# Weight-preparation jobs of the second layer in whole words, issued at the end of each tick

## The chip, the cores and the metric

The kernel runs on one core of one Trainium2 chip. The metric is the device time of one execution in microseconds (us). It uses TensorE (PE: matrix products; PEld: its weight loads), VectorE (DVE), ScalarE (ACT), GpSimd (POOL, almost unused) and SyncE (SP), whose queue issues every DMA.

## What is computed

Attention over short windows (chunks of 32 queries with 8 memory keys, 16 keys to the left, 8 to the right), then two feed-forward layers with all 3072 tokens:

```
x = attention(q, k, v, mem_k, mem_v)        # batch 4, 8 heads, 768 positions, head size 64
h = x @ w_in1;  x = softplus(h) @ w_out1    # 512 -> 2048 -> 512
h = x @ w_in2;  y = (h - tanh(h)) @ w_out2  # 512 -> 2048 -> 512
```

The weights come as 64-bit floats: in HBM each is two 32-bit words. The kernel makes a 32-bit float of the two words with integer and scaling steps, splits it in a high and a low part of a type that TensorE takes, and forms each product from three matmuls (high by high, high by low, low by high).

## The kernel before, in words

**Stages.** After an opening (the first four attention units, the first block of 512 tokens, the weights of layer 1), tokens 512 to 2047 pass layer 1 in three plain blocks: for each of 16 slices of the hidden size, `ff_h` (12 matmuls of 128x512), softplus and split (`chain1`), and, two slices later, `ff_y1` (12 matmuls). The remaining attention units run beside it. What is left (layer 1 for the last 1024 tokens, layer 2 for three groups of 1024) are four phases with a two-by-two scheme of seven products (Strassen's kind): `h_phase` is 56 groups of 6 matmuls, `y_phase` 56 groups of 6. In `y_phase` each group needs a fresh pair `gh`, `gl`: ACT casts a tile to `gh` (line 771), DVE subtracts to get `gl` (through `minus`, line 708); three such pairs can be in being at once. Here h0 and y0 are the two halves of the first phase, h1 and y1 of the second, and so on. The second phase is the first that uses the prepared weights of layer 2.

**Ticks.** `tick()` is called twice for each slice of the plain blocks and after every 12 matmuls in the phases, so a tick stands for 12 matmuls on PE, plus attention where there is any: an attention unit takes six ticks up to tick 60, then five up to tick 90. Plain blocks are ticks 0 to 97, h0 98 to 125, y0 126 to 153, h1 154 to 181, y1 182 to 209.

**Jobs.** Tables give the tick in which a job starts. A job is a generator: each tick takes it one step further. `JOBS_W1` (16 jobs) forms combinations of layer 1's weights. `JOBS_W2` (16 jobs, `job_w`) reads 1 MB of raw layer 2 weights, makes the floats, splits and stores seven combinations. `JOBS_X` (six jobs, `job_x`) reads layer 1's output, and stores seven split combinations; `JOBS_X1` is the like for layer 1. After its load, `job_w` waits `LEAD` ticks. Its steps then are: three ACT steps in one tick (lines 482, 485, 486: the low word to a 16-bit integer, the sign to a 16-bit float, the high word scaled), one DVE step that shifts and joins (488), an ACT cast of three of four parts (463), a DVE subtraction (467) and four sums (506 to 509), an ACT cast of four parts, and a DVE subtraction.

**Order.** Engines run their instructions in the order in which the program writes them. In `tick()` the jobs' steps (`active`) come before the attention's products, before softplus and cast of the current slice (`chain`), and before the copy `pT` of the transposed attention weights. Tiles named `o` rotate through four buffers: the jobs' split parts and the phases' results share them, and each is free again when its store has landed. Raw weights go to `w15`, `w6` or `w14`.

```
        active.extend(job() for job in plan.get(k, ()))
        for job in active[:]:
            if next(job, active) is active:
                active.remove(job)
        if r == 0 and before is not None:
            v_mm(before, ps_a)
```

Of the kernel before, what the change touches and what calls it, by code (L numbers as in the profile page):

```python
# [8 lines left out]
F32 = mybir.dt.float32  # L9
# [3 lines left out]
U16 = mybir.dt.uint16  # L13
F16 = mybir.dt.float16
AF = mybir.ActivationFunctionType
ALU = mybir.AluOpType
# [6 lines left out]
P = 128  # L23
# [11 lines left out]
N = 512  # L35
# [39 lines left out]
WPLACE = {q: i for i, q in enumerate((1, 2, 5, 6, 3, 7, 4))}  # L75
SHARED = {7: 7, 15: 7, 6: 14, 14: 14}
PLAIN = NB - 2
LEAD = 4
AHEAD = 3
GSLOT = (8, 9, 10, 11, 12, 13, 14, 7)  # L80
JOBS_W1 = (
    (0, "o", 7), (4, "i", 7), (8, "o", 6), (15, "i", 6), (19, "o", 0), (25, "i", 0), (30, "o", 1), (34, "i", 1),
    (40, "o", 2), (46, "i", 2), (50, "o", 3), (55, "i", 3), (60, "o", 4), (64, "i", 4), (68, "o", 5), (73, "i", 5),
)
JOBS_W2 = (
    (7, 15), (17, 15), (23, 6), (32, 15), (38, 6), (47, 15), (53, 6), (65, 15),
    (71, 6), (76, 15), (86, 15), (106, 14), (127, 15), (138, 15), (148, 15), (157, 14),
)
JOBS_X = (97, 114, 158, 168, 210, 220)
JOBS_X1 = (79, 91)  # L90
PHASES = ((1, NT - 1),) + tuple((2, b) for b in range(NT))
EXP_BIAS = 2.0 ** -112
SIGN_ONLY = 2.0 ** -100
LOW_EDGE = 2.0 ** -16
LOW_SCALE = 2.0 ** -29 * (1.0 - LOW_EDGE)
# [4 lines left out]
def attention_ffn_ffn(  # L100
# [10 lines left out]
    nc = tc.nc  # L111
    scale = 1.0 / float(D) ** 0.5

    const = ctx.enter_context(tc.tile_pool(name="const", bufs=1))
    wpool = ctx.enter_context(tc.tile_pool(name="w", bufs=1))
# [26 lines left out]
    low_bias = const.tile([P, 1], F32, name="low_bias")  # L142
# [74 lines left out]
    def run(steps):  # L217
        for _ in steps:
            pass
# [4 lines left out]
    def x_tile(j):  # L224
        if j not in xt:
            xt[j] = xpool.tile([P, KT, 2, N], F32R, name=f"x{j % 2}")
        return xt[j]
# [233 lines left out]
    def split_to(src, dst, shape):  # L461
        hi = opool.tile([P, *shape], F32R, name="o")
        nc.scalar.copy(out=hi, in_=src)  # L463
        yield
        put(hi, dst(0))
        lo = opool.tile([P, *shape], F32R, name="o")
        nc.vector.tensor_tensor(out=lo, in0=src, in1=hi.bitcast(F32), op=ALU.subtract)
        defer(put, lo, dst(1))
# [5 lines left out]
    def job_w(kind, p, slot):  # L474
        src = w2i if kind == "i" else w2o
        raw = wpool.tile([P, 4 * HALF, 2], U32, name=f"w{slot}")
        nc.sync.dma_start(out=raw.rearrange("p n two -> p (n two)"), in_=src[p].bitcast(U32))
        for _ in range(LEAD):
            yield
        lo, hi = raw[:, :, 0], raw[:, :, 1]  # L480
        x = raw.rearrange("p n two -> p (n two)").bitcast(U16).rearrange("p (n four) -> p n four", four=4)
        nc.scalar.activation(  # L482
            out=x[:, :, 0], in_=lo, func=AF.Identity, scale=LOW_SCALE, bias=low_bias
        )
        nc.scalar.mul(x[:, :, 1].bitcast(F16), hi.bitcast(F32), SIGN_ONLY)  # L485
        nc.scalar.mul(hi.bitcast(F32), hi.bitcast(F32), EXP_BIAS)
        yield
        nc.vector.scalar_tensor_tensor(
            out=hi, in0=hi, scalar=3, in1=lo, op0=ALU.logical_shift_left, op1=ALU.bitwise_or
        )  # L490
        yield
        w = raw.bitcast(F32)[:, :, 1].rearrange("p (i n) -> p i n", i=4)

        def place(s, a, n):
            return wid[p][:, a : a + n, s] if kind == "i" else wod[1][:, a : a + n, p, s]

        yield from split_to(
            w[:, 1:4], lambda s: ((0, 2, place(s, 0, 2)), (2, 1, place(s, 6, 1))), [3, HALF]
        )
        sums(w)  # L500
        yield
        yield from split_to(w, lambda s: ((0, 4, place(s, 2, 4)),), [4, HALF])

    def sums(w):
        add, sub = ALU.add, ALU.subtract
        nc.vector.tensor_tensor(out=w[:, 0], in0=w[:, 0], in1=w[:, 3], op=add)
        nc.vector.tensor_tensor(out=w[:, 1], in0=w[:, 0], in1=w[:, 1], op=sub)
        nc.vector.tensor_tensor(out=w[:, 2], in0=w[:, 2], in1=w[:, 1], op=sub)
        nc.vector.tensor_tensor(out=w[:, 3], in0=w[:, 3], in1=w[:, 1], op=sub)
# [68 lines left out]
        yield  # L578
        low(4, b21)

    def job_x(b, e):
        raw = wpool.tile([P, 2, 2, N], F32, name="w15")
        nc.sync.dma_start(out=raw, in_=y1d[b][e])
        for _ in range(LEAD):
            yield
        b11, b21, b12, b22 = raw[:, 0, 0], raw[:, 0, 1], raw[:, 1, 0], raw[:, 1, 1]
        o = {}

        def high(q, src):
            if b and q in (2, 5, 7):  # L590
                h, l = (gpool.tile([P, N], F32R, name=n) for n in ("gh", "gl"))
                stores = [(x2d[b][q - 1][:, e, s], t) for s, t in enumerate((h, l))]
            else:
                t = opool.tile([P, 2, N], F32R, name="o")
                h, l = t[:, 0], t[:, 1]
                stores = [(x2d[b][q - 1][:, e], t)]
            o[q] = h, l, src, stores
            nc.scalar.copy(out=h, in_=src)

        def low(q):  # L600
            h, l, src, stores = o.pop(q)
            minus(l, src, h.bitcast(F32))
            for place, t in stores:
                defer(nc.sync.dma_start, place, t.bitcast(F32))

        high(1, b11)
        high(2, b21)
        yield
        low(1)
        low(2)  # L610
        minus(b12, b12, b11)
        high(3, b22)
        yield
        low(3)
        minus(b22, b22, b12)
        high(5, b12)
        yield
        low(5)
        minus(b11, b22, b11)
        high(6, b22)  # L620
        yield
        low(6)
        minus(b21, b21, b22)
        high(7, b11)
        yield
        low(7)
        high(4, b21)
        yield
        low(4)
# [77 lines left out]
    def minus(out, x, y):  # L707
        nc.vector.tensor_tensor(out=out, in0=x, in1=y, op=ALU.subtract)  # L708
# [118 lines left out]
    slot = 0  # L827
# [7 lines left out]
    plan, now, active, late = {}, [0], [], []  # L835
# [2 lines left out]
        plan.setdefault(t, []).append(lambda x=(kind, p): job_w1(*x))  # L838
    for (t, slot), w in zip(JOBS_W2, W2):
        plan.setdefault(t, []).append(lambda x=(*w, slot): job_w(*x))  # L840
    for n, t in enumerate(JOBS_X):
        plan.setdefault(t, []).append(lambda x=(n // 2, n % 2): job_x(*x))
    for n, t in enumerate(JOBS_X1):
        plan.setdefault(t, []).append(lambda n=n: job_x1(n))
    starts = {t: i for i, t in enumerate((*ATT_TICKS, AT_END))}
# [3 lines left out]
    def defer(f, *args, more=0):  # L849
        late.append((now[0] + more, f, args))  # L850

    def tick(chain=iter(())):
        k = now[0]
        now[0] += 1
        calls, late[:] = [x for x in late if x[0] <= k], [x for x in late if x[0] > k]
        for _, f, args in calls:
            f(*args)
        if k in starts:
            place[:] = starts[k], k
        i, r = place[0], k - place[1]  # L860
        u = ATT_ORDER[i] if i < len(ATT_ORDER) else None
        before = ATT_ORDER[i - 1] if 0 < i <= len(ATT_ORDER) else None
        if u is not None:
            if r == 1:
                if i + 2 < len(ATT_ORDER):
                    qk_load(ATT_ORDER[i + 2])
                if 0 < i < len(ATT_ORDER) - 1:
                    v_load(ATT_ORDER[i + 1])
                next(soft[u])
            elif r == 2:  # L870
                run(soft.pop(u))
        if r == 1 and before in VIA_DRAM:
            run(soft.pop(("x", before)))
        active.extend(job() for job in plan.get(k, ()))
        for job in active[:]:
            if next(job, active) is active:
                active.remove(job)
        if r == 0 and before is not None:
            v_mm(before, ps_a)
        if r == 0 and u is not None:  # L880
            s_mm(u, ps_a)
        if r == 4 and u is not None:
            t_mm(u, ps_a[:, 0, :])
        next(chain, None)
        if r == 4 and u is not None:
            t_out(u)
        next(chain, None)
        if r == 0 and before is not None:
            soft["x", before] = (x_out if before // UB < PLAIN else x_out_whole)(before)
            next(soft["x", before])  # L890
        if r == 0 and u is not None:
            soft[u] = softmax(u)
            next(soft[u])
        if r == 0 and before is not None:
            next(soft["x", before], None)
        run(chain)

    with tc.manual_schedule(engines={mybir.EngineType.PE}):

# [9 lines left out]
        if True:  # L909
# [6 lines left out]
            for name in ORDER.split():  # L916
                kind, i = name.rstrip("0123456789"), int(name.lstrip("qkviow"))
# [23 lines left out]
            for token in OPENING.split():  # L941
                op = token[:2] if token[0] == "c" else token.rstrip("0123456789")
                i = int(token[len(op) :])
# [5 lines left out]
                elif op == "Z":  # L949
                    for _ in range(i):  # L950
                        nc.tensor.matmul(
                            out=ps_h[1], lhsT=zeros[:, :P], rhs=zeros, start=True, stop=True
# [23 lines left out]
                else:  # L976
                    if op == "y":
                        going["w", i] = split_w(raws[str(i)], i)
                    elif op[0] == "y":
                        k = "io".index(op[1])  # L980
# [8 lines left out]
        for j in range(1, PLAIN):  # L989
            x = x_tile(j)  # L990
# [108 lines left out]
```

## Time and profile before

| | |
|---|---|
| median of three runs | 1093.36 us (1091.57 to 1097.41) |
| profiled execution: its own time | 1098.39 us |
| profiled execution: span, first to last instruction | 1096.5 us |
| PE / DVE / ACT busy | 1054.6 / 751.5 / 677.2 us |
| mean granted TensorE clock | 0.978 of full speed |
| DMA | 319.99 MB, mean 292 GB/s |

The page is of one execution. Its own time is 1.9 us more than its span, and 5.0 us more than the median of the three runs. Busy time of PE counts a product from its start to its modelled end, so it overlaps its neighbours; what PE loses is better read from the distance between rows of the same work.

### The profile page before, as it was taken

To read this page: it belongs to the slowest core of one execution; us is meant where nothing else is said; L and a number is where in the kernel's file an instruction comes from. 1 tells how busy PE (TensorE), PEld (TensorE's weight loads), DVE (VectorE), ACT (ScalarE), POOL (GpSimd) and SP (SyncE) were. 2 spreads that over 40 slices of the span, in tenths; PEclk is the share of its full clock that TensorE was granted. 3 is DMA by queue.
4 is the path that set the end of the run, shared out by engine and by line. 5 is a ranking of instruction groups with operands and counts; after the bars stand their busy time and mean duration, and the time that the engine had idled before them with its cause. 6 is when DMAs were issued, how large, how long until landed. Compare 5 with 4: busy or idle time off the path is not lost.

```text
span 1096.5 us, 18583 instructions
## 1 busy us (share of the span) xinstructions
PE 1054.6 (96%) x7322; PEld 858.3 (78%) x7322; DVE 751.5 (69%) x1199; ACT 677.2 (62%) x982; POOL 7.5 (1%) x14
## 2 busy tenths in 40 slices
PE   7999999998999988999988998999999999999998
PEld 5787888887787866878866776878888888888887
DVE  7997557667686564555675667887678677455876
ACT  6996566977787785557566574555455554344553
POOL 1000000000000000000000000000000000000000
PEclk8999999999899898999998998999999999999999
DMA  9999877797799873699987999988889878655661
GB/s 378 408 323 328 287 255 243 245 342 257 269 312 320 296 241 130 240 392 341 371 321 298 362 350 356 332 320 306 314 290 375 313 289 327 233 199 211 217 215 68
DMA packets 112231, 319.99 MB, mean 292 GB/s; under 512 B 8464, under 2 KB 67344, under 8 KB 93712
## 3 DMA queue, kind: packets, MB, share of 16 engines
q1 hardware_dynamic: 112144, 318.80, 81.1%
q8 instruction: 58, 0.95, 0.3%
q14 instruction: 29, 0.24, 0.1%
HBM read 220.73 MB, written 98.04 MB: 291 GB/s over the span
## 4 chain that ended last, share of the span: by engine, by line
PE 80%; ACT 10%; DVE 5%; DMA 3%; issue 2%; SPq 0%; ACTq 0%; DVEq 0%
PE ps_y L404 40%; PE ps_h L404 24%; PE ps_b L404 12%; ACT w L482 2%; ACT w L485 2%; PE ps_a L367 2%; PE ps_a L286 1%; DMA wod<-o 1%; DMA x<-wid 1%; PE ps_a L338 1%; ACT o L463 1%; DVE w L708 1%; ACT t L427 1%; ACT gh L771 1%; ACT gh L439 1%
## 5 line engine op out<-in xcount | busy, mean ns | idle before, releaser
L771 ACT CAST gh<-w 128x512 fp32r<-128x512 f32 x224 | 138.9, 624 | 137.7 <-DVE gl L708 99.9
L708 DVE TENSOR_TENSOR gl<-w,gh 128x512 fp32r<-128x512 f32 x236 | 162.7, 691 | 77.1 <-ACT gh L771 71.7
L404 PE MATMUL ps_h<-x,w 128*128 128x512 f32 x756 | 183.3, 393 | 0.1
L404 PE MATMUL ps_y<-gh,w 128*128 128x512 f32 x512 | 174.9, 404 | 0.0
L404 PEld LDWEIGHTS ps_h<-x,w 128*128 128x128 f32 x756 | 142.1, 189 | 30.2 <-ACT t L427 0.2
L404 PE MATMUL ps_y<-w,x 128*128 128x512 f32 x504 | 122.7, 396 | 3.7 <-ACT kept L699 3.7
L404 PE MATMUL ps_y<-gh,x 128*128 128x512 f32 x384 | 119.5, 389 | 0.4 <-ACT gh L771 0.4
L404 PEld LDWEIGHTS ps_y<-w,x 128*128 128x128 f32 x504 | 96.5, 192 | 24.8 <-ACT kept L699 4.5
L404 PEld LDWEIGHTS ps_y<-gh,w 128*128 128x128 f32 x512 | 98.1, 192 | 21.9 <-issue 0.2
L404 PE MATMUL ps_y<-gl,w 128*128 128x512 f32 x256 | 101.4, 396 | 0.0
L404 PEld LDWEIGHTS ps_y<-gh,x 128*128 128x128 f32 x384 | 72.1, 188 | 15.7 <-ACT gh L771 0.8
L735 ACT ACTIVATE tanh<-sum 128x512 f32<-128x512 f32 x72 | 45.3, 633 | 57.5 <-DVE sum L704 57.4
L404 PE MATMUL ps_b<-gh,x 128*128 128x512 f32 x192 | 75.0, 390 | 4.0 <-ACT gh L771 4.0
L404 PE MATMUL ps_y<-gl,x 128*128 128x512 f32 x192 | 74.9, 390 | 0.2 <-DVE gl L708 0.2
L444 DVE TENSOR_TENSOR gl<-t,gh 128x512 fp32r<-128x512 f32 x64 | 45.5, 714 | 43.1 <-ACT gh L439 42.9
L404 PE MATMUL ps_h<-gh,x 128*128 128x512 f32 x192 | 74.9, 390 | 0.0
L404 PE MATMUL ps_b<-w,x 128*128 128x512 f32 x252 | 64.3, 391 | 2.1 <-ACT kept L699 1.3
L708 DVE TENSOR_TENSOR w<-w 128x512 f32<-128x512 f32 x88 | 60.4, 688 | 6.6 <-ACT w L427 5.4
L404 PE MATMUL ps_h<-w,x 128*128 128x512 f32 x252 | 64.1, 390 | 0.3 <-DMA x<-wid 0.3
L427 ACT ACTIVATE t<-ps_h 128x512 f32<-128x512 f32 x64 | 38.1, 596 | 39.6 <-PE ps_h L404 36.2
L704 DVE TENSOR_TENSOR sum<-ps_y,kept 128x512 f32<-128x512 f32 x48 | 32.9, 690 | 41.7 <-PE ps_y L404 32.1
L404 PEld LDWEIGHTS ps_b<-w,x 128*128 128x128 f32 x252 | 47.1, 188 | 13.0 <-ACT kept L699 2.2
(161 smaller groups left out, 1720.5 us busy)
## 6 DMA issues: line engine op xcount, KB each, us to landing
x<-wod SPq DMA_DIRECT2D x48, 1024.0 KB, 5.0
x<-wid SPq DMA_DIRECT2D x24, 1024.0 KB, 7.2
w<-x2d SPq DMA_DIRECT2D x21, 1024.0 KB, 7.3
x<-wid SPq DMA_DIRECT2D x24, 768.0 KB, 6.8
wod<-o SPq DMA_DIRECT2D x32, 512.0 KB, 5.8
wid<-o SPq DMA_DIRECT2D x32, 512.0 KB, 5.5
qk<-in_qk SPq DMA_DIRECT2D x21, 768.0 KB, 6.4
x2d<-o SPq DMA_DIRECT2D x30, 512.0 KB, 8.8
```

Of the source, the lines that this page charges most:

```text
L286: nc.tensor.matmul(out=ps[cc, j, KEYS * p : KEYS * (p + 1)], lhsT=a["q"][r, p, cc], rhs=a["k"][r, c, p, :], start=True, stop=True,)
L338: nc.tensor.transpose(ps[:, p * P : (p + 1) * P], a["sm"][:, p * P : (p + 1) * P], ident)
L367: nc.tensor.matmul(out=ps[h : h + 64, p % 2, 2 * P + t0 : 2 * P + t0 + CHUNK], lhsT=v, rhs=pT, start=True, stop=True,)
L404: nc.tensor.matmul(out=ps, lhsT=a, rhs=b, start=first and i == 0, stop=last and i == 2, skip_group_check=on,)
L427: nc.scalar.activation(out=out, in_=x, func=AF.Softplus)
L444: eng.tensor_tensor(out=gl, in0=t, in1=gh.bitcast(F32), op=ALU.subtract)
L482: nc.scalar.activation(out=x[:, :, 0], in_=lo, func=AF.Identity, scale=LOW_SCALE, bias=low_bias)
L485: nc.scalar.mul(x[:, :, 1].bitcast(F16), hi.bitcast(F32), SIGN_ONLY)
L704: nc.vector.tensor_tensor(out=h, in0=ps, in1=t, op=ALU.add)
L708: nc.vector.tensor_tensor(out=out, in0=x, in1=y, op=ALU.subtract)
L735: nc.scalar.activation(out=t, in_=h, func=AF.Tanh)
L771: nc.scalar.copy(out=gh, in_=src)
```

## The change

Each raw pair of words is now made to a float by two ACT steps and two DVE steps, one in each of four ticks, all on whole 32-bit words: ACT turns the low word to its three bits in place; DVE joins the sign bit from the high word to it; ACT scales the high word; DVE shifts it and joins the two. The wait after a load is three ticks and not four, for `job_x` too. A further tick without a step stands between the first split and the second. The jobs' block moves to the end of `tick()`. The tables get new ticks, and `job_x` and one `job_w` other raw buffers (`w7`, `w10`).

```
-LEAD = 4
+LEAD = 3
...
 JOBS_W2 = (
...
-    (71, 6), (76, 15), (86, 15), (106, 14), (127, 15), (138, 15), (148, 15), (157, 14),
+    (67, 6), (73, 15), (90, 10), (96, 15), (107, 14), (111, 15), (127, 15), (149, 15),
 )
-JOBS_X = (97, 114, 158, 168, 210, 220)
+JOBS_X = ((85, 15), (105, 7), (157, 7), (163, 15), (210, 15), (220, 15))
...
         lo, hi = raw[:, :, 0], raw[:, :, 1]
-        x = raw.rearrange("p n two -> p (n two)").bitcast(U16).rearrange("p (n four) -> p n four", four=4)
-        nc.scalar.activation(
-            out=x[:, :, 0], in_=lo, func=AF.Identity, scale=LOW_SCALE, bias=low_bias
+        nc.scalar.activation(out=lo, in_=lo, func=AF.Identity, scale=LOW_SCALE, bias=low_bias)
+        yield
+        nc.vector.scalar_tensor_tensor(
+            out=lo, in0=hi, scalar=0x80000000, in1=lo, op0=ALU.bitwise_and, op1=ALU.bitwise_or
         )
-        nc.scalar.mul(x[:, :, 1].bitcast(F16), hi.bitcast(F32), SIGN_ONLY)
+        yield
         nc.scalar.mul(hi.bitcast(F32), hi.bitcast(F32), EXP_BIAS)
         yield
         nc.vector.scalar_tensor_tensor(
...
         sums(w)
+        yield
         yield
...
-    def job_x(b, e):
-        raw = wpool.tile([P, 2, 2, N], F32, name="w15")
+    def job_x(b, e, slot):
+        raw = wpool.tile([P, 2, 2, N], F32, name=f"w{slot}")
...
-        active.extend(job() for job in plan.get(k, ()))
-        for job in active[:]:
-            if next(job, active) is active:
-                active.remove(job)
         if r == 0 and before is not None:
             v_mm(before, ps_a)
...
         run(chain)
+        active.extend(job() for job in plan.get(k, ()))
+        for job in active[:]:
+            if next(job, active) is active:
+                active.remove(job)
```

One thing more follows from the code. The loops that fill the plan use the name `slot`, which also numbers the plain blocks' two PSUM banks; it leaves them at 14 before and at 15 now, so the first plain slice takes bank `ps_h[1]` and not `ps_h[0]`, and all later slices swap too.

**ACT in y0.** The order of ACT's instructions around the job that starts in tick 127, before (its raw tile is `w_5621`; `gh` are the casts that PE waits for, `kept` copies of finished products):

```order
L699 COPY kept<-ps_h_81 128x512
L771 CAST gh<-w_5271 128x512
L771 CAST gh<-w_5280 128x512
L771 CAST gh<-w_5419 128x512
L482 ACTIVATE w_5621<-w_5621,low_bias 128x1024
L485 ACTIVATE w_5621<-w_5621 128x1024
L486 ACTIVATE w_5621<-w_5621 128x1024
L771 CAST gh<-w_5428 128x512
```

and now (raw tile `w_5669`; line 773 is the line 771 of before, 487 is 486):

```order
L773 CAST gh<-w_5317 128x512
L481 ACTIVATE w_5669<-w_5669,low_bias 128x1024
L773 CAST gh<-w_5326 128x512
L773 CAST gh<-w_5478 128x512
L773 CAST gh<-w_5487 128x512
L773 CAST gh<-w_5572 128x512
L487 ACTIVATE w_5669<-w_5669 128x1024
L773 CAST gh<-w_5572 128x512 x3
```

Three job steps stood between two casts; now one does, twice, with four casts between them.

**ACT in the plain blocks.** The same around the ninth of these jobs (started in tick 71 before, 67 now), which falls beside attention (`t` is softplus, `pT` the copy that the attention's last products wait for, `o<-c` a step of a `JOBS_W1` job). Before:

```order
L427 ACTIVATE t<-ps_h_82 128x512
L350 COPY pT<-ps_a 128x512
L439 CAST gh<-t 128x512
L482 ACTIVATE w_4128<-w_4128,low_bias 128x1024
L485 ACTIVATE w_4128<-w_4128 128x1024
L486 ACTIVATE w_4128<-w_4128 128x1024
L463 CAST o<-c_4177 128x1024
L387 COPY x_3903<-ps_a 128x2x2x128
```

Now:

```order
L387 COPY x_3911<-ps_a 128x2x2x128
L463 CAST o<-w_3735 128x1024
L481 ACTIVATE w_3972<-w_3972,low_bias 128x1024
L327 ACT_TABLE_LOAD
L327 ACTIVATE sm<-sm 128x512
L427 ACT_TABLE_LOAD
L427 ACTIVATE t<-ps_h_82 128x512
L439 CAST gh<-t 128x512
L487 ACTIVATE w_3972<-w_3972 128x1024
L463 CAST o<-c_4113 128x1024
```

The attention's copy to `x` now stands ahead of the jobs' steps of its tick, and the two conversion steps are a tick's work apart.

**DVE in y0.** What DVE gets for it around the same job of y0 (`gl` is the subtraction that PE waits for). Before:

```order
L708 TENSOR_TENSOR gl<-w_5419,gh 128x512
L708 TENSOR_TENSOR gl<-w_5428,gh 128x512
L708 TENSOR_TENSOR w_5519<-w_5280 128x512
L708 TENSOR_TENSOR gl<-w_5518,gh 128x512
L488 SCALAR_TENSOR_TENSOR w_5621<-w_5621 128x1024
```

Now:

```order
L710 TENSOR_TENSOR gl<-w_5478,gh 128x512
L483 SCALAR_TENSOR_TENSOR w_5669<-w_5669 128x1024
L710 TENSOR_TENSOR gl<-w_5487,gh 128x512
L710 TENSOR_TENSOR w_5573<-w_5326 128x512
L710 TENSOR_TENSOR gl<-w_5572,gh 128x512 x2
L710 TENSOR_TENSOR w_5573<-w_5478 128x512
L710 TENSOR_TENSOR gl<-w_5572,gh 128x512
L798 TENSOR_TENSOR o<-ps_b_4861,kept 128x512
L489 SCALAR_TENSOR_TENSOR w_5669<-w_5669 128x1024
```

One step of 1024 elements has become two, with seven instructions of the phase between them.

## Rows read from the trace of the kernel before

**Rows 1.** The page: span, and busy time of each engine.

```profile
span 1096.5 us, 18583 instructions
...
PE 1054.6 (96%) x7322; PEld 858.3 (78%) x7322; DVE 751.5 (69%) x1199; ACT 677.2 (62%) x982; POOL 7.5 (1%) x14
```

**Rows 2.** Busy by stage: window, length, PE, PEld, DVE, ACT, POOL; granted clock, DMA share, GB/s.

```profile
127.00:324.00 197.00, 192.38 (x2060) 157.53 (x2042) 135.37 (x245) 146.47 (x161) 0.00 (x0) 0.98 0.81 276
324.00:455.00 131.00, 121.10 (x1183) 98.97 (x1174) 81.37 (x143) 92.34 (x108) 0.00 (x0) 0.95 0.70 237
455.00:532.00 77.00, 76.60 (x336) 62.47 (x335) 41.74 (x65) 48.37 (x78) 0.00 (x0) 1.00 0.98 363
532.00:625.00 93.00, 83.86 (x340) 65.97 (x339) 63.92 (x100) 54.36 (x72) 0.00 (x0) 0.94 0.90 333
625.00:711.00 86.00, 80.36 (x340) 65.29 (x339) 62.52 (x99) 54.88 (x83) 0.00 (x0) 0.96 0.95 349
```

**Rows 3.** The chain of waits in order of time: start us, length us, what.

```profile
127.19 2.99 PE ps_y L404 x12
...
146.13 2.96 PE ps_y L404 x12
...
324.10 2.97 PE ps_y L404 x12
...
513.48 19.04 PE ps_y L404 x84
...
625.14 19.04 PE ps_y L404 x84
...
710.65 1.38 PE ps_y L404 x6
...
1016.65 76.17 PE ps_y L404 x336
```

**Rows 4.** Timeline of PE: the first group of h0.

```profile
454.92 1.53 PE L404 MATMUL ps_b<-w,ring 128*128 128x512 f32 x6
```

**Rows 5.** Timeline of ACT in y0: start, length; in brackets idle before, releaser.

```profile
549.40 2.60 ACT L482 ACTIVATE w<-w,low_bias 128x1024 uint16<-128x1024 uint32 x1
552.03 2.48 ACT L485 ACTIVATE w<-w 128x1024 f16<-128x1024 f32 x1
...
555.55 1.65 ACT L771 CAST gh<-w 128x512 fp32r<-128x512 f32 x3
```

**Rows 6.** Timeline of PE at the same place.

```profile
556.21 0.50 PE L404 MATMUL ps_b<-gh,x 128*128 128x512 f32 x1 [3.29 <-ACT gh L771]
```

**Rows 7.** Groups by line and shape: count, busy us, mean ns, idle before.

```profile
L482 ACT ACTIVATE w<-w,low_bias 128x1024 uint16<-128x1024 uint32 x16 | 41.9, 2621 | 1.0 <-DMA w<-in_w2o 1.0
L485 ACT ACTIVATE w<-w 128x1024 f16<-128x1024 f32 x16 | 40.3, 2516 | 0.5
...
L488 DVE SCALAR_TENSOR_TENSOR w<-w 128x1024 uint32<-128x1024 uint32 x16 | 19.6, 1223 | 26.8 <-ACT w L486 26.8
...
L486 ACT ACTIVATE w<-w 128x1024 f32<-128x1024 f32 x16 | 18.1, 1129 | 0.5
...
L467 DVE TENSOR_TENSOR o<-w,o 128x768 fp32r<-128x768 f32 x16 | 15.2, 952 | 0.3
...
L506 DVE TENSOR_TENSOR w<-w 128x256 f32<-128x256 f32 x16 | 6.7, 420 | 0.0
...
L177 ACT ACTIVATE c<-w,low_bias 128x1024 uint16<-128x1024 uint32 x4 | 5.8, 1453 | 0.0
```

**Rows 8.** The loads of raw weights (line 477): time from issue to landing.

```profile
DMA to landing us min/median/max: 6.6/8.6/11.4
```

**Rows 9.** Timeline of ACT late in y0: a job's cast that waits for a store.

```profile
607.47 1.12 ACT L463 CAST o<-w 128x1024 fp32r<-128x1024 f32 x1 [3.98 <-DMA wod<-o]
```

**Rows 10.** Waits of PE: total us, times, longest us.

```profile
PE ps_a L338 <- DVE sm L333: 8.0, 5, 2.9
```

**Rows 11.** Five microseconds of y0 (columns as in rows 2).

```profile
580.00:585.00 5.00, 5.00 (x23) 4.13 (x22) 3.54 (x6) 3.25 (x6) 0.00 (x0) 1.00 1.01 428
```

More of the change, by code (lines that the diff above doesn't have):

```diff
@@ L81 @@
 JOBS_W1 = (
-    (0, "o", 7), (4, "i", 7), (8, "o", 6), (15, "i", 6), (19, "o", 0), (25, "i", 0), (30, "o", 1), (34, "i", 1),
-    (40, "o", 2), (46, "i", 2), (50, "o", 3), (55, "i", 3), (60, "o", 4), (64, "i", 4), (68, "o", 5), (73, "i", 5),
+    (0, "o", 7), (4, "i", 7), (8, "o", 6), (12, "i", 6), (16, "o", 0), (20, "i", 0), (24, "o", 1), (29, "i", 1),
+    (35, "o", 2), (40, "i", 2), (44, "o", 3), (48, "i", 3), (52, "o", 4), (61, "i", 4), (70, "o", 5), (75, "i", 5),
 )
 JOBS_W2 = (
-    (7, 15), (17, 15), (23, 6), (32, 15), (38, 6), (47, 15), (53, 6), (65, 15),
-    (71, 6), (76, 15), (86, 15), (106, 14), (127, 15), (138, 15), (148, 15), (157, 14),
+    (5, 15), (17, 15), (23, 6), (31, 15), (38, 6), (46, 15), (51, 6), (60, 15),
+    (67, 6), (73, 15), (90, 10), (96, 15), (107, 14), (111, 15), (127, 15), (149, 15),
 )
-JOBS_X = (97, 114, 158, 168, 210, 220)
+JOBS_X = ((85, 15), (105, 7), (157, 7), (163, 15), (210, 15), (220, 15))
 JOBS_X1 = (79, 91)
@@ L840, in attention_ffn_ffn @@
         plan.setdefault(t, []).append(lambda x=(*w, slot): job_w(*x))
-    for n, t in enumerate(JOBS_X):
-        plan.setdefault(t, []).append(lambda x=(n // 2, n % 2): job_x(*x))
+    for n, (t, slot) in enumerate(JOBS_X):
+        plan.setdefault(t, []).append(lambda x=(n // 2, n % 2, slot): job_x(*x))
     for n, t in enumerate(JOBS_X1):
```

## The prediction

> **What bounds the kernel now.** The page comes first: PE is busy for 1054.6 of 1096.5 us, ACT for 677.2 and DVE for 751.5 [rows 1]. So only PE can be the bound as a whole, and 1096.5 - 1054.6 = 41.9 us of idle is what one sees at once. It isn't all that PE loses. The table by stage shows where: in the plain blocks, in y0 and in h1 PE has 4.6, 9.9, 9.1 and 5.6 us idle, and in the same four stages the granted clock is 0.94 to 0.98, while h0 stands at 1.00 with 0.4 us idle [rows 2]. A clock below 1.00 as a mean of a stage is time at the lower of its two levels (1.2 GHz in place of 2.4): products run, but slower.
>
> To have both losses in one number I use the pace of undisturbed work. The last half phase is 336 matmuls in 76.17 us [rows 3], so 0.227 us each, 2.72 us for a tick's 12, 76.17 us for each half phase. Against that:
> - Plain blocks: from 127.19 to the start of h0 at 454.92 [rows 3, 4] are 327.7 us. Without loss they are ten attention units of six ticks, 146.13 - 127.19 = 18.94 each; six of five ticks, one tick less, 16.22 each; and at the end seven groups of 12 matmuls, 19.0. That makes 305.7. Lost: 22.0. By tick 60 (324.10 in place of 127.19 + 189.4 = 316.6) 7.5 of it have gone, the rest after.
> - h0: 454.92 to 532.52 (513.48 + 19.04): 77.6, lost 1.4. y0: to 625.14, 92.6, lost 16.4. h1: to 710.65, 85.5, lost 9.3 [rows 3, 4].
> - The next four halves: 710.65 to 1016.65 are 306.0, against 304.7: lost 1.3. The last half loses nothing.
>
> In all 22.0 + 1.4 + 16.4 + 9.3 + 1.3 = 50.4 us: idle, and the slow clock behind it.
>
> **What causes it.** One place in y0 shows the pattern: ACT runs lines 482 and 485 from 549.40, then 486, and casts the next `gh` only at 555.55: a hold of 6.15 us [rows 5]. PE starts again at 556.21, after 3.29 us of idle whose releaser is that `gh` [rows 6]. So in y0 a hold of about 6.15 - 3.29 = 2.9 us is covered by the pairs that are ready, and what is over it, PE pays. The three steps cost 2621 + 2516 + 1129 = 6266 ns by their means, in 16 jobs [rows 7]. The two that write 16-bit halves of words take more than twice the one that writes whole words, for 1024 elements each.
>
> **The change part by part.** *Removed:* lines 482 and 485, 5.14 us of ACT per job. *Added:* one ACT step from integer words to integer words, in place, and one DVE step. The trace has no ACT step of this form. From below, the nearest is line 486, also whole words in place: 1.13 us; a step of less is excluded since it handles as many elements. From above it is line 482 itself, same function and input: 2.62 us; in between stands line 177, which writes the same integers to another tile: 1.45 us [rows 7]. I take 1.2, near 486, because the two rows at 2.5 share only the half-word writing in place. By the Trainium skill (ScalarE: Activation LUTs, "What ACT_TABLE_LOAD costs") an activation with a bias tile takes some 280 + 0.833 x 1024 = 1133 ns, whatever the type: an estimate that leaves my sum as it is. For the half-word steps the trace contradicts it, 2621 measured; were it right there too, the old burst would be some 3.4 us and hardly worth breaking up.
>
> So a job's conversion takes 1.2 + 1.13 = 2.3 us of ACT in place of 6.3, in two ticks. The longest hold by one conversion step falls from 6.3 to 1.2 us, well under the 2.9 of cover. DVE gains 1.22 us per job (as line 488 [rows 7]), 16 x 1.22 = 19.6 us over the kernel, beside 345 us in which it is idle.
>
> *Moved to the end of the tick:* softplus, casts, `pT` and the attention's copies no longer stand behind the jobs' steps of the same tick. In the plain blocks this takes from attention the waits that came through ACT. The price is that jobs run a little later; all that they make is stored ticks before it is read (the last `JOBS_W2` job ends in tick 161, and y1, its reader, starts in tick 182), so I cost this at nothing. The same holds for the additional empty tick.
>
> *Three ticks after a load instead of four:* three ticks are 8.2 us, loads land after 6.6, 8.6 and 11.4 us (least, median, most) [rows 8]. ACT may so be held between 0 and 3.2 us per job, 0.4 at the median. That is at the 2.9 us of y0 in the worst case and nearly always under it: between 0 and 16 x 0.3 = 5 us; I take 1.
>
> *New ticks and buffers.* Jobs leave y0: three started there, now two, one of them with all but two steps in h1. h0 gets more: `JOBS_W2` jobs from 96, 107 and 111 and one `job_x`, where one and two were. In h0 ACT is idle for 28.6 and DVE for 35.3 of 77 us [rows 2], so it has room. The other PSUM bank for the first plain slice costs nothing: between the last use of that bank and the first slice PE has the groups Y12 and Y13 of the opening, 5.4 us, to hide one softplus; without them it would be less than a microsecond, once.
>
> *What is late next.* Three kinds of wait remain. A job's second cast waits for an `o` whose store hasn't landed: 3.98 us at 607.47 [rows 9], over the cover; the empty tick (2.7 us) takes most of it, but h1 holds a `JOBS_W2` job and two `job_x` end to end. DVE's longest step is still a subtraction and four sums in one tick, 0.95 + 4 x 0.42 = 2.6 us [rows 7]. And attention waits for DVE's `sm`, 8.0 us in five places [rows 10]. I leave 1.5 us in the plain blocks, 2 in y0 (the load's 1 in it) and 2 in h1; 1.4 of h0 and 1.3 behind y1's start stay, since nothing there is taken away.
>
> **Sum.** Recovered: 22.0 - 1.5 = 20.5; 16.4 - 2 = 14.4; 9.3 - 2 = 7.3; together 42.2. The profiled execution took 1098.4, which gives **1056.2**. Its time was 5.0 above the median of 1093.4; the work without loss, 1098.4 - 50.4 = 1048.0, is the same in each run, so I take the runs' spread for spread of the stalls that go, and forecast **1056 us** for the median.
>
> **Rivals.**
> 1. *The integer step costs 2.6 us after all* (what is slow is the integer input or being in place). For it: line 482 has both. Against: line 485 has no integer and is as slow. Then one hold of 2.6 us per job, just under the cover; with a cast or a store behind it some spill, up to 1 us for half of the 16 jobs: 1058 to 1064. Chance 0.12.
> 2. *DMA bounds h0.* It moved 363 GB/s x 77 us = 28.0 MB [rows 2]. By the tile shapes a `JOBS_W2` job is 2.9 MB and a `job_x` 4.7, so two jobs and a half more and one `job_x` less add about 2.9: 30.9 MB in 76.2 us, 405 GB/s. Five microseconds of y0 reached 428 [rows 11], so it can fit, but stores will land later, and `o` waits with them. If it holds only 363, h0 takes 30.9 / 0.363 = 85 us, 9 more than its products: 1060 to 1068. Chance 0.17. By the Trainium skill (DMA: Bandwidth & Descriptors, "Where 436 GB/s comes from") HBM gives a core some 358 GB/s: h0 would then take 86 us, 10 more than its products. The 428 of rows 11 speak against that as a ceiling here.
> 3. *DVE becomes the wait.* Jobs now overlap in the plain blocks, and a tick can hold a first split (2.6 us) beside the four sums of a `JOBS_W1` job (1.7): 4.3 us in ticks 13 and 25, with little less in 71, 75 and 81. `sm` comes late, at up to 2.9 us [rows 10] in each of five places: 14.5, less the 1.5 already left in, 1069. For it: DVE is the busiest engine after PE. Against: two ticks lie between attention's DVE steps and PE's use. Chance 0.10.
> 4. *Slower: each load holds ACT.* With three ticks' lead, the first conversion step waits at the head of ACT's queue, now without other work between. Once loads take over 8.2 + 6.3 - 1.2 = 13.3 us, the hold is longer than today's burst and every stall is back, larger. At 17 us the hold is 10 us, 3.7 more than now, in 16 jobs 59 us more: about 1150. It decides from 13.3 us; the longest landing now is 11.4 [rows 8]. Chance 0.03.
> 5. *The stalls hardly move,* because each only passes to the next engine in its chain: 1090 to 1096. Against: rows 5 and 6 name one cause. Chance 0.02.
>
> **How the numbers follow.** The forecast has 0.56, with a range of its own of 1049 to 1062 (nothing left of the losses in y0, h1 and the plain blocks gives 1050.7, the runs' spread a little less). About 0.5% (5.5 us) is what a measurement of this kernel can tell from no change. Faster by that: forecast and rivals 1 to 3, 0.95; same 0.02; slower 0.03. For eight in ten the range starts at 1047 and takes in rivals 1 and 2 and rival 3: to 1073.
>
> **What would show it.** Right: the new ACT step at 1.1 to 1.5 us; no wait of PE on `gh`, `pT` or `kept` over 1 us in y0, h1 or the plain blocks; the granted clock at 1.00 in the plain blocks from the second on and in y0 and h1; y0 and h1 at 76 to 79 us; the plain blocks, tick 0 to h0, at about 307. Wrong: h0 over 80 us with casts that wait for stores (rival 2); PE waiting for `sm` over 10 us in all (rival 3); ACT waiting for raw loads at the step (rival 4).

## The result, and the profile after

The changed kernel takes 1057.18 us (median of four runs, 1054.88 to 1057.76) against 1093.41 before (median of four runs too): a ratio of 0.966, 95% interval 0.963 to 0.969. The forecast was 1056, with a range of 1047 to 1073. The profiled execution took 1054.88 us with a span of 1053.1, against 1098.39 and 1096.5. The two profiled executions lie 43.5 us apart and the medians 36.2: the one before was 5.0 above its median, this one is 2.3 below. Stage by stage the text reads the profiles.

The page after, in the lines that answer to [rows 1], and the granted clock in 40 slices:

```profile
span 1053.1 us, 18599 instructions
...
PE 1034.4 (98%) x7320; PEld 846.0 (80%) x7322; DVE 768.8 (73%) x1215; ACT 615.8 (58%) x966; POOL 7.9 (1%) x14
...
PEclk9999999999999999999999999999999999999999
```

ACT lost 61.4 us of work, DVE gained 17.3. PE's idle time fell from 41.9 to 18.7 us, and the granted clock is 0.9 or more in each of the 40 slices.

The chain of waits in order of time, at the places of [rows 3] (start, length, what):

```profile
125.21 2.99 PE ps_y L404 x12
...
494.17 19.04 PE ps_y L404 x84
...
590.41 19.04 PE ps_y L404 x84
...
668.43 76.16 PE ps_y L404 x336
...
973.24 76.17 PE ps_y L404 x336
```

The timeline of PE has h0's first group, as [rows 4] before:

```profile
430.57 1.52 PE L404 MATMUL ps_b<-w,ring 128*128 128x512 f32 x6
```

By the pace used in the prediction (305.7 us from tick 0 to h0, 76.2 for each half phase) the plain blocks now take 305.4 and lose nothing; h0, to 494.17 + 19.04 = 513.21, takes 82.6 and loses 6.4; y0 takes 77.2 and loses 1.0; h1 78.0, 1.8; the four halves after it 304.8, 0.1. Losses before were 22.0, 1.4, 16.4, 9.3 and 1.3. So 50.4 us of loss have become 9. Another 2 us lie ahead of tick 0, which starts at 125.21 and not at 127.19; in the kernels below it starts at 125.0 to 127.5, with the change or parts of it, so these 2 us are chance. Four of the five stages gave up most or all of their loss; h0 lost more than before.

Busy time by stage, columns as in [rows 2], with the new borders (plain blocks, h0, y0, h1, the rest):

```profile
125.00:431.00 306.00, 305.48 (x3237) 250.81 (x3219) 233.41 (x406) 199.84 (x264) 0.00 (x0) 1.00 0.84 290
431.00:513.00 82.00, 78.16 (x335) 63.56 (x334) 50.77 (x77) 49.47 (x79) 0.00 (x0) 0.98 1.02 385
513.00:590.00 77.00, 76.53 (x336) 62.75 (x336) 60.47 (x94) 41.36 (x65) 0.00 (x0) 1.00 0.97 360
590.00:668.00 78.00, 76.73 (x337) 62.92 (x336) 59.07 (x93) 44.77 (x76) 0.00 (x0) 1.00 0.92 346
668.00:1053.00 385.00, 381.40 (x1682) 315.24 (x1681) 267.92 (x414) 187.19 (x315) 0.00 (x0) 1.00 0.74 262
```

Of these five only h0 has a clock under 1.00, and it moves the most data: 385 GB/s at a DMA share of 1.02. That is 31.6 MB in 82 us, where [rows 2] give 28.0 in 77.

The new steps, groups by line and shape (481 and 487 on ACT, 483 on DVE), for [rows 7]:

```profile
L481 ACT ACTIVATE w<-w,low_bias 128x1024 uint32<-128x1024 uint32 x16 | 19.8, 1237 | 5.2 <-DMA w<-in_w2i 4.5 <-DMA w<-in_w2o 0.6
...
L483 DVE SCALAR_TENSOR_TENSOR w<-w 128x1024 uint32<-128x1024 uint32 x16 | 19.5, 1220 | 0.8 <-ACT w L481 0.8
L487 ACT ACTIVATE w<-w 128x1024 f32<-128x1024 f32 x16 | 18.5, 1155 | 7.1 <-DVE w L483 6.9
```

The integer step takes 1.24 us. What is left of PE's waits (total, times, longest):

```profile
PE ps_b L404 <- ACT kept L701: 3.6, 1, 3.6
...
PE ps_a L338 <- DVE sm L333: 1.3, 1, 1.3
```

The longest stands in h0. The timeline of ACT shows what is ahead of it, and that of PE the wait itself:

```profile
474.18 0.62 ACT L600 CAST o<-w 128x512 fp32r<-128x512 f32 x1 [6.41 <-DMA wod<-o]
```

```profile
478.43 1.86 PE L404 MATMUL ps_b<-w,x 128*128 128x512 f32 x6 [3.60 <-ACT kept L701]
```

A `job_x` cast waits 6.41 us for an `o` tile whose store (of the job begun in tick 96) hasn't landed; behind it on ACT stands the copy `kept` that frees PE's bank. It is the kind of wait of [rows 9].

### The profile page after: what moved, and what is told of

It is laid out like the page before. It is cut to its first block, busy times and chain, and to the rows that moved or that the text cites. A ratio compares the mean times of both kernels' runs of the same rounds, so it can differ in the third digit from the quotient of the medians.

```text
span 1053.1 us, 18599 instructions
## 1 busy us (share of the span) xinstructions
PE 1034.4 (98%) x7320; PEld 846.0 (80%) x7322; DVE 768.8 (73%) x1215; ACT 615.8 (58%) x966; POOL 7.9 (1%) x14
## 4 chain that ended last, share of the span: by engine, by line
PE 89%; DMA 6%; ACT 2%; DVE 2%; issue 1%; SPq 0%; ACTq 0%
PE ps_y L404 43%; PE ps_h L404 29%; PE ps_b L404 13%; DMA x<-wid 3%; PE ps_a L367 2%; PE ps_a L286 1%; DMA wod<-o 1%; DMA v<-in_vv 1%; DMA w<-in_w1o 1%; PE ps_a L338 1%; DVE gl L710 0%; DVE w L710 0%; ACT o L173 0%; DVE gl L444 0%; ACT t L427 0%
## 5 line engine op out<-in xcount | busy, mean ns | idle before, releaser
L404 PE MATMUL ps_y<-gh,w 128*128 128x512 f32 x512 | 171.8, 397 | 0.0
L404 PE MATMUL ps_y<-w,x 128*128 128x512 f32 x504 | 119.8, 389 | 0.9 <-DMA x<-wid 0.9
```

What stands on the lines that cost most here:

```text
L404: nc.tensor.matmul(out=ps, lhsT=a, rhs=b, start=first and i == 0, stop=last and i == 2, skip_group_check=on,)
```

## The experiments

Theory: PE stalled because one job held ACT for 6.3 us at a stretch, more than the work that lies ready for PE covers ("length of the hold"; what it covers is called the cover). Rivals: the jobs' place in the tick; crowding, that is jobs that meet each other in the same ticks; the amount of ACT work. Then, for what is left in h0: bytes, or the four `o` buffers.

The table gives the medians, the ratio to the kernel before with its interval, and the loss of each stage, read from the timeline of PE as above (distance of the first groups, less 305.7 or 76.2). The ratio is to runs of the kernel before beside each (medians of 1090.9 to 1093.8). The losses are of one profiled execution each, up to 3.2 us from its median, 5.0 for the kernel before; so a loss of one us or less decides nothing:

| kernel | us | ratio | plain | h0 | y0 | h1 | y1 |
|---|---|---|---|---|---|---|---|
| before | 1093.4 | 1 | 22.1 | 1.3 | 16.5 | 9.3 | 1.3 |
| changed | 1057.2 | 0.966 (0.963 to 0.969) | -0.3 | 6.3 | 1.0 | 1.8 | 0.0 |
| steps only | 1068.8 | 0.977 (0.976 to 0.979) | 1.8 | 8.9 | 2.9 | 8.7 | 1.3 |
| order only | 1098.3 | 1.005 (1.003 to 1.006) | 20.8 | 3.6 | 16.4 | 9.2 | 1.3 |
| halves apart | 1066.1 | 0.976 (0.974 to 0.979) | 4.0 | 10.9 | 2.4 | 1.3 | 0.0 |
| burst, new ticks | 1096.2 | 1.003 (1.001 to 1.005) | 16.2 | 23.3 | 6.4 | 1.3 | 0.0 |
| job_x on gh/gl | 1055.6 | 0.967 (0.965 to 0.970) | 0.0 | 4.6 | 1.0 | 1.7 | 0.0 |
| four ticks' lead | 1056.7 | 0.968 (0.965 to 0.970) | 1.4 | 6.1 | 0.5 | 1.4 | 0.0 |
| no empty tick | 1066.3 | 0.977 (0.974 to 0.979) | 7.4 | 8.7 | 1.1 | 1.6 | 0.0 |
| less in h0 | 1071.0 | 0.979 (0.977 to 0.981) | 18.1 | 2.7 | 1.1 | 1.6 | 0.0 |
| less in h0, gh/gl | 1070.8 | 0.980 (0.977 to 0.983) | 16.5 | 1.9 | 1.9 | 1.5 | 0.0 |
| spread to y0 | 1057.0 | 0.966 (0.964 to 0.969) | 0.2 | 2.2 | 4.8 | 1.5 | 0.0 |

### Steps only

The new body of the conversion in the kernel before, and nothing else:

```
-        nc.scalar.activation(out=x[:, :, 0], in_=lo, ...)
-        nc.scalar.mul(x[:, :, 1].bitcast(F16), hi.bitcast(F32), SIGN_ONLY)
+        nc.scalar.activation(out=lo, in_=lo, func=AF.Identity, scale=LOW_SCALE, bias=low_bias)
+        yield
+        nc.vector.scalar_tensor_tensor(out=lo, in0=hi, scalar=0x80000000, in1=lo, ...)
+        yield
         nc.scalar.mul(hi.bitcast(F32), hi.bitcast(F32), EXP_BIAS)
```

> The kernel before with nothing but the four whole-word steps (old ticks, four ticks' lead, jobs ahead in the tick). Theory 'length of the hold': PE stalled because ACT was held 6.3 us at a stretch; now no step holds it over 1.3 us, so most of the gain comes with this alone: y0 at 78 to 80 us, h1 at 78 to 81, the whole at 1057 to 1066. Rival 'place in the tick': in the plain blocks the stalls come from jobs standing ahead of softplus and of the attention copies, and stay: plain blocks lose 10 us or more, the whole 1068 to 1080. Rival 'crowding': what helps is that jobs left y0 and no longer meet each other; then y0 and h1 keep over half of their losses (16.4 and 9.3 us) and the whole stays over 1075.

Measured: 1068.8 us, 24 of the 36 us of gain, and over the theory's 1057 to 1066. y0 lost 2.9 in place of 16.5 and the plain blocks 1.8 in place of 22.1: those two are the steps' doing, and neither place in the tick nor crowding was needed. But h1 kept 8.7 of 9.3, and h0 lost 8.9. By stage (h0, y0, h1; columns as in [rows 2]):

```profile
433.00:518.00 85.00, 78.60 (x338) 63.95 (x337) 44.01 (x67) 44.55 (x77) 0.00 (x0) 0.98 0.93 338
518.00:597.00 79.00, 77.25 (x338) 62.69 (x336) 64.87 (x101) 45.02 (x69) 0.00 (x0) 1.00 0.98 369
597.00:682.00 85.00, 79.35 (x338) 64.65 (x337) 65.25 (x101) 47.72 (x80) 0.00 (x0) 0.96 0.99 362
```

What h1 keeps is the meeting of the job of tick 157 with the `job_x` of tick 158. In its chain stands, once the burst is gone:

```profile
627.34 10.01 DMA x2d<-o
...
637.37 0.96 DVE o L467
```

A store of 10 us holds an `o` back, and the job's subtraction with it. The theory's 78 to 81 us for h1 was wrong; in h1 the rival 'crowding' holds.

In h0, which has none of the new ticks' bytes here (338 GB/s in 85 us, 28.7 MB), half of the loss is a wait of PE for a load of `x`:

```profile
PE ps_h L404 <- DMA x<-wid: 4.7, 1, 4.7
```

So h0 can lose as much without more to move. Why that load is late wasn't tested.

### Order only

```
+        (the jobs' block of tick(), moved behind run(chain))
```

> The kernel before with the jobs' block moved to the end of the tick and nothing else. Theory 'length of the hold': in y0 and h1 a tick has no chain behind the jobs, so nothing moves there (y0 at 90 to 93 us, h1 at 83 to 86), and the plain blocks, where the hold of 6.3 us only comes a little later, keep most of their 22 us: 1080 to 1096. Rival 'place in the tick': the plain blocks lose under 8 us and the whole is at 1075 to 1080.

Measured: 1098.3, slightly slower than before. 20.8 of the 22.1 us in the plain blocks stay. PE's waits in the plain blocks, in the kernel before:

```profile
PE ps_a L367 <- ACT pT L350: 7.8, 3, 4.0
PE ps_a L338 <- DVE sm L333: 6.7, 4, 2.9
```

and here:

```profile
PE ps_a L338 <- DVE sm L333: 9.1, 4, 6.1
PE ps_a L367 <- ACT pT L350: 5.7, 4, 2.1
PE ps_a L338 <- ACT t L427: 2.8, 2, 2.2
```

`pT` gains 2.1 us, `sm` loses 2.4, and 2.8 for softplus (`t`) are new. My reading is that the burst, now behind the chain of its own tick, meets the next tick's. Moving a hold doesn't shorten it. What the new order gives on top of the short steps wasn't run by itself.

### Halves apart

The changed kernel with the old half-word steps, one in each tick:

```
         nc.scalar.activation(out=x[:, :, 0], in_=lo, ...)
+        yield
         nc.scalar.mul(x[:, :, 1].bitcast(F16), hi.bitcast(F32), SIGN_ONLY)
+        yield
         nc.scalar.mul(hi.bitcast(F32), hi.bitcast(F32), EXP_BIAS)
         yield
```

> The changed kernel with the old half-word steps, but each in a tick of its own (2.6, 2.5 and 1.1 us on ACT, then the DVE step), so that a job is as many ticks long as now. Theory 'length of the hold': a hold of 2.6 us is under the 2.9 us of cover in y0, so it costs little: 1056 to 1063, no wait of PE for a cast over 1 us in y0. Rival 'ACT work': what counts is the 4 us of ACT that each job saves, and giving it back costs a good part of the gain: over 1068.

Measured: 1066.1, between the two ranges. In y0, where the theory was to be tested, PE waits for no `gh`, and the stage loses 2.4 us. The 16.5 before were of three such jobs, and here one whole job runs in y0; so the fair measure is the next kernel, with the same ACT work at the same ticks, but in one stretch: it loses 6.4. The length of the hold counts, not the sum of work. The rest is in h0 (10.9 in place of 6.3) and 4.0 in the plain blocks, where the steps come behind other waits. From the chain in h0:

```profile
469.07 12.41 DMA wod<-o
...
486.48 2.37 ACT w L486
```

The wait for the store is there in the changed kernel too; here steps of 2.5 and 2.6 us stand in the same line behind it, and PE waits 7.1 us in place of 3.6. A hold adds to the hold ahead of it.

### Burst, new ticks

The changed kernel with the three old ACT steps in one tick, and two empty ticks behind them.

```
         nc.scalar.mul(hi.bitcast(F32), hi.bitcast(F32), EXP_BIAS)
         yield
+        yield
+        yield
```

> The changed kernel with the old three ACT steps in one tick (6.3 us), two empty ticks after them, new ticks and order. Theory 'length of the hold': each job that starts in y0 stalls PE again by about 6.2 - 2.9 = 3.3 us and a fall of the clock (two such jobs: some 10 us), and the plain blocks lose some of their 22 us again: 1070 to 1085. Rival 'crowding': the new ticks are what helps, and it stays under 1063.

Measured: 1096.2. The new ticks and the new order, without the new steps, are worth nothing. I expected 1070 to 1085: the one whole job in y0 cost 6.4, more than half of the 10 thought for two, but I hadn't counted h0, where the bursts of three jobs now fall: it loses 23.3. h1 loses 1.3 even with the burst, where the short steps alone at the old ticks left 8.7. PE's waits from tick 0 to h1's end:

```profile
PE ps_b L404 <- ACT kept L702: 13.3, 3, 8.7
PE ps_a L338 <- ACT t L427: 7.2, 2, 4.1
...
PE ps_b L404 <- ACT gh L774: 3.3, 1, 3.3
```

The 3.3 us is y0's and equals [rows 6]. Together with the run before it shows that the new ticks suit short steps only. The other 12 us came on top of the steps by ticks, order, buffers, lead and empty tick together; for lead and empty tick see below, the others weren't parted.

### The cover, measured

The changed kernel with 1 to 7 ACT steps of 1.05 us at a stretch on a scratch tile, in the last two y phases:

```
+    HOLDS = {243: 1, 248: 2, 253: 3, 258: 4, 299: 5, 306: 6, 313: 7}
...
+        for _ in range(HOLDS.get(k, 0)):
+            nc.scalar.mul(scratch[0], scratch[0], 1.0)
```

> The changed kernel with rows of idle work on ACT of about 1.05 us each put in seven ticks of the two last y phases, where PE loses nothing: 1, 2, 3, 4, 5, 6 and 7 of them at a stretch, on a scratch tile. Theory 'cover of 2.9 us': PE idles for 0, 0, 0.3, 1.3, 2.4, 3.5 and 4.5 us behind them (a hold less 2.9), after the longer ones with products at half clock. If the cover is smaller, the first waits show at one or two; if casts can catch up further, later.

It took 1078.0 us in its one run. The timeline of ACT shows the last three rows of steps with their lengths, that of PE the waits behind them:

```profile
994.83 5.41 ACT L908 ACTIVATE w<-w 128x1024 f32<-128x1024 f32 x5
...
1018.64 6.50 ACT L908 ACTIVATE w<-w 128x1024 f32<-128x1024 f32 x6
...
1044.66 7.59 ACT L908 ACTIVATE w<-w 128x1024 f32<-128x1024 f32 x7
```

```profile
1000.80 0.49 PE L404 MATMUL ps_y<-gh,x 128*128 128x512 f32 x1 [2.46 <-ACT gh L773]
...
1025.70 0.79 PE L404 MATMUL ps_y<-gh,x 128*128 128x512 f32 x1 [3.55 <-ACT gh L773]
1052.81 0.79 PE L404 MATMUL ps_y<-gh,x 128*128 128x512 f32 x1 [4.63 <-ACT gh L773]
```

Hold less wait is 2.95, 2.95 and 2.96 us; the hold of four steps (4.33, wait 1.37) gives 2.96 too. Holds of one and two left no wait; the one of three (3.24) left 0.77 where 0.3 was expected, so a cover of 2.5 there. The cover read from one row in the prediction, 2.9, comes back at four of the five places where PE waited; it isn't the same at every place.

### job_x on gh/gl, and four ticks' lead

```
-            if b and q in (2, 5, 7):
+            if (b or e) and q in (2, 5, 7):
```

> The changed kernel; in the job_x that runs in h0, three of seven split tiles take the gh/gl buffers that lie idle in h0, and not the four o buffers (the job_x of later phases do this already). Theory 'o and the stores': h0's 6.3 us come from ACT waiting 6.4 us for an o whose store has not landed; without that wait h0 is at 77 to 79 us and the whole some 4 us under the changed kernel, 1050 to 1055. Rival 'DMA bytes': h0 has too much to move, and the wait only passes to the loads of wid or to the next store: h0 stays over 81 and the whole within 1.5 us of the changed kernel.

```
-LEAD = 3
+LEAD = 4
```

> The changed kernel with four ticks' lead after a load. If three ticks cost ACT waits that reach PE, this is faster by 1 to 3 us; by the trace of the changed kernel ACT waited 5.2 us in all for raw loads, none of it in a chain that reached PE, so I expect no difference from the changed kernel beyond 1.5 us (1055 to 1059), unless the later steps meet others.

The first: 1055.6, no difference that the intervals show, and h0 loses 4.6 in place of 6.3. ACT's 6.4 us for an `o` are gone from h0's chain; in their place ACT waits for a raw load, and the chain goes from there through `kept` to PE:

```profile
ACT w L481 <- DMA w<-in_w2o: 4.7, 1, 4.7
```

So neither theory as stated: h0 stands at 80.7 us, over the 79 of the one and under the 81 of the other. The wait passed on to the next transfer, as the rival had it; the buffer alone is not the cause. The second: 1056.7, as expected. ACT's wait for raw loads shrinks from 5.2 to 1.6 us, and the whole gains nothing that the intervals show:

```profile
L481 ACT ACTIVATE w<-w,low_bias 128x1024 uint32<-128x1024 uint32 x16 | 19.7, 1233 | 1.6 <-DMA w<-in_w2o 1.6
```

### No empty tick

```
         sums(w)
         yield
-        yield
```

> The changed kernel without the empty tick between first and second split. Theory 'o and the stores': the second cast comes 2.7 us earlier, nearer to the store that frees its o, so ACT waits more: 1 to 6 us slower (1058 to 1063), in h0 and y0. Rival: the tick is idle padding, no difference within 1.5 us.

Measured: 1066.3, more than expected; y0, where some of it was expected, loses what it lost. The larger part, 7.4 us, is in the plain blocks, where I had not looked: a job's cast meets the store of a finished block's results (`y1d`) in the `o` buffers and waits 8.1 us for it; ACT's order carries that on to the attention's copy behind it, DVE's order to `sm`, and PE waits:

```profile
PE ps_a L338 <- DVE sm L333: 5.0, 1, 5.0
```

### Less in h0, less with gh/gl, and spread to y0

One start less in h0 and one more at tick 10; then with the `job_x` of h0 on gh/gl as well; then without the start at tick 10, but with one job more in y0:

```
-(90, 10), (96, 15), (107, 14), (111, 15), (127, 15), (149, 15),
+(10, 6), ... (90, 10), (96, 15), (111, 15), (127, 15), (149, 15),     # the first two
+(90, 10), (96, 15), (111, 15), (124, 15), (137, 15), (149, 15),       # the third
```

> The changed kernel with one JOBS_W2 job less in h0: the jobs of tick 107 on move up, and a new start stands at tick 10 (buffer w6). Theory 'DMA bytes in h0': h0 loses 6.3 us because the 16 DMA engines have too much there (share 1.01, 379 GB/s); 2.9 MB less brings h0 to 77 to 79 us, the wait of 6.4 us on a store goes, and the whole is 3 to 5 us under the changed kernel: 1051 to 1055. Rival 'o alone': the job_x still meets the stores of the job of tick 96 in the four o buffers, and h0 stays over 80.

> The same with the job_x of h0 on gh/gl buffers too. If bytes are the cause and o only where they show, this adds under 1.5 us to the run before; if both count, h0 is at 76 to 77 and the whole at 1049 to 1052, the least that the pace of undisturbed work allows.

> The changed kernel with the job of tick 107 taken out of h0 to the other side: starts at 96, 111, 124, 137 and 149 in place of 96, 107, 111, 127 and 149, and the job_x of h0 on gh/gl buffers. No start in the plain blocks moves, so the stall that the start at tick 10 made there should be gone (plain blocks lose under 1 us). Theory 'DMA bytes in h0': h0 loses 2 to 3 us in place of 6.3; y0, now with two whole jobs, loses 2 to 3 in place of 1, since no hold of ACT goes over the cover; the whole at 1052 to 1056, 1 to 4 us under the changed kernel. Rival: the job only carries its stall along, and y0 loses as much as h0 gains: 1056 to 1059.

With one job less h0 loses 2.7, with gh/gl 1.9, and in the third 2.2, in place of 6.3. That fits the bytes theory (2.9 MB less), and 'o alone' is out; but ACT still waits 4.5 us for a store in the first, where that wait was to go, and a job takes its own steps and `o` tiles along with its bytes, which no run parts. And none is faster: 1071.0, 1070.8 and 1057.0, the first two far off what I expected. The start at tick 10 cost 16 to 18 us in the plain blocks: three jobs of this kind and two of `JOBS_W1` overlap there, and ACT and DVE queue behind stores that land after 9.6 and 11.5 us. PE's longest wait, and the two stores in the chain of the first of these kernels:

```profile
PE ps_h L404 <- ACT t L427: 9.5, 1, 9.5
```

```profile
183.54 9.63 DMA wid<-o
...
207.24 11.50 DMA wod<-o
```

In the third, y0 takes up 3.8 us as h0 gives 4.1: its rival was right. In y0 DVE is the busier engine, and PE waits for subtractions as well as casts there:

```profile
543.62 0.50 PE L404 MATMUL ps_b<-gl,x 128*128 128x512 f32 x1 [0.31 <-DVE gl L710]
558.31 0.50 PE L404 MATMUL ps_b<-gh,x 128*128 128x512 f32 x1 [1.02 <-ACT gh L773]
```

These waits are 2.5 us in all and don't account for the whole 4.8. None of the twelve kernels is measurably faster than the changed one.

### What made the old steps slow

Eight single ACT steps of 1024 elements in the changed kernel's last y phase (code shortened). The pitch is the distance from one written element to the next:

```
+            ident32(four(a)[:, :, 0])              # halves in place, 8-byte pitch
+            ident32(four(b)[:, :, 0])              # another tile, 8-byte pitch
+            ident32(halves(b)[:, :1024])           # another tile, packed
+            ident32(b[:, :, 0])                    # words, 8-byte pitch
+            ident32(b ... [:, :1024])              # words, packed
+            (f16 <- f32 in another tile: 8-byte pitch, packed, 4-byte pitch)
```

> The changed kernel with eight single ACT instructions on a scratch tile in the last y phase, 1024 elements each, to see what makes the old steps slow: integer words to 16-bit halves in place (8-byte pitch), to another tile at the same pitch, to another tile packed; to words of another tile at 8-byte pitch and packed; float words to 16-bit halves in another tile at 8-byte pitch, packed, and at 4-byte pitch. If single halves written at a pitch of 8 bytes are slow as such, those at 8 bytes take 2.5 to 2.6 us in another tile too; if it is only being in place, they fall to about 1.4. Words should take 1.1 to 1.25. One tick holds at most 2.6 us, so PE should lose nothing.

The timeline of ACT, in that order:

```profile
996.36 2.61 ACT L913 ACTIVATE w<-w,low_bias 128x1024 uint16<-128x1024 uint32 x1
1002.16 2.62 ACT L913 ACTIVATE w<-w,low_bias 128x1024 uint16<-128x1024 uint32 x1
1007.98 1.23 ACT L913 ACTIVATE w<-w,low_bias 128x1024 uint16<-128x1024 uint32 x1
1013.43 1.22 ACT L913 ACTIVATE w<-w,low_bias 128x1024 uint32<-128x1024 uint32 x1
1018.87 1.23 ACT L913 ACTIVATE w<-w,low_bias 128x1024 uint32<-128x1024 uint32 x1
1024.31 2.53 ACT L927 ACTIVATE w<-w 128x1024 f16<-128x1024 f32 x1
1030.04 1.14 ACT L929 ACTIVATE w<-w 128x1024 f16<-128x1024 f32 x1
1035.48 1.39 ACT L931 ACTIVATE w<-w 128x1024 f16<-128x1024 f32 x1
```

Halves at a pitch of 8 bytes cost twice, in place or not, from integers or floats; packed halves cost what words cost, and words cost the same at either pitch. That PE would lose nothing did not come out: from the first product of this last phase to the end are 81.1 us (976.59 to 1057.7), where the changed kernel has 80.0 (973.08 to 1053.1). Products start late by about 0.3 us in all behind each of the three steps of 2.5 and 2.6 us, and nowhere else. So a single step of that length is at the edge of the cover, not safely under it.

## Why the prediction was right, point by point

**What bounded the kernel.** Right. The loss by stage, read against the pace of undisturbed work, was what could be had: 41 of 50.4 us came back in the profile, 42.2 were forecast. The medians moved by 36.2. That fits the prediction's reading that the 5.0 us by which the profile before lay over its median are stalls that go; it isn't shown by itself.

**The cause.** Right and shown for y0 and the plain blocks: with short steps alone they give up their losses (2.9 and 1.8 us stay); at the new ticks the same ACT work costs them 2.4 and 4.0 us in steps apart, 6.4 and 16.2 in one burst. The cover is 2.95 us at most places, read as 2.9. For h1 it wasn't the cause: short steps alone leave 8.7 of its 9.3 us, and the burst at the new ticks leaves 1.3. The 7.3 us that the sum recovers there came, but by the new ticks and what came with them (order alone leaves 9.2), to which the prediction had given no share of the sum; that term is right by luck.

**The integer step.** Taken as 1.2, it takes 1.24; rival 1 falls. The reason given ("the two rows at 2.5 share only the half-word writing in place") was half right: it is the 8-byte pitch of the halves, not being in place. The rule of the Trainium skill (ScalarE: Activation LUTs, "What ACT_TABLE_LOAD costs") gives an estimate of 1.13 us for 1024 elements with a bias tile, for fp32 and bf16 alike; the prediction's "whatever the type" goes further than that. It lies 0.1 under the integer words and packed integer halves measured here (1.22 to 1.24), and is off by more than a factor of two for integer halves at an 8-byte pitch (2.61).

**The place in the tick.** Wrong as far as it was given a share. "In the plain blocks this takes from attention the waits that came through ACT" isn't so by itself: order alone left 20.8 of 22.1 us. The forecast had put no separate sum on it; what it gives beside short steps stays open.

**The lead of three ticks.** Costed at 1 us, in y0; no cost clear of the runs' spread was found: with four ticks the kernel takes 1056.7, and y0 loses 0.5 in place of 1.0.

**What is late next.** The term that was mis-sized is h0: "1.4 of h0 and 1.3 behind y1's start stay, since nothing there is taken away". h0 lost 6.3. "So it has room" was read from ACT's and DVE's idle time; what lacked room was the transfers and the `o` buffers that wait for them. Rival 2 had this mechanism, but as another case and not as a part of the likeliest one, and its sign, h0 over 80 us with casts that wait for stores, came true beside a right forecast. Its bytes were too few: two jobs and a half at 2.9 MB less 4.7 are 2.6 and not 2.9, and the rows give 3.6 more. By its 363 GB/s h0 would have taken 85 us; it took 82.6, at 385 GB/s. That is above the 358 that the Trainium skill gives as a core's limit from HBM (DMA: Bandwidth & Descriptors, "Where 436 GB/s comes from"); here one core ran alone. One job less brings h0's loss to 2.7; but bytes aren't all of it, since the steps alone lose 8.9 in h0 without them. Against that, the plain blocks lost nothing where 1.5 was left, y0 1.0 where 2 was, and y1 nothing where 1.3 was. That 1.3 went with the new ticks (it stays with the steps alone and with the order alone, and is gone in every kernel with the new ticks). These misses of 1 to 5 us cancel: 8.2 us were left in the sum, 9 stayed. That the sum is better than its terms is luck.

**Rivals 3 to 5.** PE waits 1.3 us for `sm`, all of it in the opening, as before; ACT waits 5.2 us for raw loads, and none of it is in a chain that reached PE (with `job_x` on gh/gl 4.7 us in h0 are); and the stalls went. None came in. What became of the DVE step in a crowded tick can't be told from these runs, since ticks 13 and 25 lost nothing.

## What to carry to other kernels

An engine that feeds the bound one in a fixed order does harm by its longest stretch more than by its sum: measure the cover (the hold less the wait; here 2.95 us at most places and 2.5 at one), and cut side work in pieces that stay well under it. Look at the time of an instruction for each form before counting elements: words, or packed halves, where halves at a wide pitch cost twice. When side work is moved, count the bytes that it brings to the stage where it lands, and see whose buffers its stores share; each new place that I tried gave its gain back, in h0, y0 or the plain blocks.

## What the runs showed that was not expected

An empty tick between two casts of a job was worth 9 us (1066.3 against 1057.2), though the job does nothing in it: without it a cast in the plain blocks waits 8.1 us for a store, with it 2.3. A job started at tick 10, in a stage where PE lost nothing, cost 16 to 18 us. And ACT writes 1024 16-bit halves at an 8-byte pitch in 2.6 us, at 4 bytes in 1.4, packed in 1.1 to 1.2.
